# Sparse attention and four attention experts: 64-query blocks with one 120-row contraction, heads in pairs, batched small operations, stationary weights in the projections

## The chip, the cores and the metric

The kernel runs on one core of a Trainium2 chip. The metric is device time in microseconds of one launch; the kernel before took 674.88 us, the median of three runs (674.37 to 676.24). The engines are PE (matrix multiplications; it takes a stationary operand by a weight load and streams a moving one past it), DVE, ACT and POOL (elementwise work), and SP, which here only issues DMAs. Each engine has its own instruction stream and waits for others on semaphores. PE writes to PSUM, a small memory that DVE and ACT read.

## The reference

Two parts in sequence. The first is attention for 4 batches, 8 heads, 768 positions and 64 dimensions. Each query sees the keys less than 16 positions away, and 24 summaries of 32 keys each (the maximum of the keys, the mean of the values), whose scores get log(32) added:

```
k_sum = k.reshape(B, H, nb, block, D).max(axis=3)
v_sum = v.reshape(B, H, nb, block, D).mean(axis=3)
mask_l = np.abs(pos[:, None] - pos[None, :]) < window
scores_s = scale * np.einsum('bhsd,bhnd->bhsn', q, k_sum)
scores_s = scores_s + np.log(block)
scores_all = np.concatenate([scores_l_m, scores_s], axis=-1)
return np.matmul(a, v_all).astype(np.float32)
```

Its output, heads side by side, is x: 4 batches of 768 rows of 512. The second part picks two of four experts per row and adds their causal attention (64 dimensions each), weighted:

```
logits = x @ w_gate
topk = np.argpartition(-logits, K, axis=-1)[..., :K]
for e in range(E):
    q = x @ wq[e]; k = x @ wk[e]; v = x @ wv[e]
    ye = a @ v @ wo[e]
    out += mask[..., None] * w[:, :, kk:kk + 1] * ye
```

All four experts are computed for all rows, and the weight of an expert that isn't picked is zero. Since the choice compares logits, x has to be exact: both kernels compute the first part's values in f32 and carry x as the sum of two f16 numbers.

## The kernel before

**Stage 1** (L117 to L253) runs over batches and, inside, over four pairs of heads, and is done for all four batches before stage 2 begins. Per head: q, k and v are loaded (POOL issues q and k with a cast to f16, SP or ACT issues v in f32). PE transposes q and k, six tiles of 128 positions each (L145, L147), with 64 useful columns out of 128. Twelve records, six f32 matmuls with an indicator matrix (L155), give the sums of v over blocks of 32. For each tile of 128 queries there are two score matmuls: against the 128 keys of the tile itself (L182, mask by POOL, L193 and L195), and against a second set of 128 rows, `kT_B`, that holds neighbours of the tile and the 24 summaries (L185, mask by DVE, L197). ACT takes the exponential of both (L189). Two f32 matmuls of 128 stationary columns and 65 moving ones (64 values and a one for the sum of weights) add up the values (L205, L207); DVE and ACT divide, and split the result into a high and a low f16 part (L210 to L222). The twelve tiles of both parts are transposed (L238 to L248).

**Stage 2** (L255 to L402) runs per batch: the gate for each tile (thirteen small operations on 128 x 4 numbers), and for two pairs of experts the projection with x as stationary operand (L318), eviction, transposes of q and k (L327, L329), causal scores (L343), exponentials (L346, POOL clears above the diagonal), values (L357), division and weighting (L361 to L364); at the end the output projection (L392, L394) and the store.

**Order.** The program is written with a framework that orders the instructions of each engine by priority and readiness in its own model, sets semaphores, and hands out buffers from pools; a tile allocated again waits for the readers of the earlier one. PE's order in stage 1 interleaves the values of one head with the transposes and scores of the next. The number of buffers is written at each tile (`bufs=`).

## Time and profile before

| | us |
|---|---|
| median of three runs | 674.88 |
| lowest, highest | 674.37, 676.24 |
| span of the profiled execution | 676.0 |
| PE busy | 575.3 (85%) |
| DVE busy | 342.3 (51%) |
| ACT busy | 296.3 (44%) |
| POOL busy | 256.4 (38%) |

The profile is of one execution, whose own time is its span; it lies 1.1 us above the median. Busy shares are averages over both stages. The first stage ends at about 441 us. A matmul is pipelined: its duration contains the passage through the array, so what a matmul costs in a row of them is read from the distance of starts. A row of the timeline that merges several (x6) spans from the first start to the last end; less the duration of one, divided by their number less one, it gives that distance. An f32 matmul leaves two records, so x12 are six of them.

### The profile page before, as it was taken

How to read it: one execution, taken by the hardware profiler on the slowest of the kernel's cores; microseconds unless marked ns; L12 is line 12 of the kernel's file. 1: busy time of each engine (PE TensorE's matmuls, PEld its weight loads, DVE VectorE, ACT ScalarE, POOL GpSimd, SP SyncE). 2: the span in 40 equal slices, each digit the busy share in tenths (PEclk: the TensorE clock that was granted, in tenths of full speed). 3: DMA queues.
4: the chain of work that ended last, by engine and by line, in shares of the span. 5: the costliest groups of instructions: out<-in, count | busy, mean ns of one | idle time of the engine just before them, and what ended most of it. 6: DMA issues, size and time to landing. Idle time of an engine off the chain costs nothing.

```text
span 676.0 us, 10937 instructions
## 1 busy us (share of the span) xinstructions
PE 575.3 (85%) x3248; PEld 426.8 (63%) x3248; DVE 342.3 (51%) x1797; ACT 296.3 (44%) x958; POOL 256.4 (38%) x813
## 2 busy tenths in 40 slices
PE   1998999899998998999999898877887897797874
PEld 1887887788777877887778777653343343333331
DVE  0455554554554545545455455556565457447443
ACT  1444444444443444444444444434643643543541
POOL 9877453554544535545444243310210210210120
PEclk9999999999999999999999999999776566655655
DMA  5977241332322413323231010000001002002002
GB/s 66 60 67 60 36 35 18 35 39 23 30 24 37 36 17 34 39 25 29 25 42 19 13 24 1 1 1 0 1 33 62 1 1 95 0 1 84 12 1 93
DMA packets 85962, 20.63 MB, mean 31 GB/s; under 512 B 82576, under 2 KB 82832, under 8 KB 85904
## 3 DMA queue, kind: packets, MB, share of 16 engines
q0 software_dynamic: 56832, 7.35, 16.8%
q1 hardware_dynamic: 14800, 6.30, 3.4%
q10 hardware_dynamic: 14272, 6.29, 3.3%
q8 instruction: 26, 0.43, 0.3%
q14 instruction: 32, 0.26, 0.1%
HBM read 20.98 MB, written 6.29 MB: 40 GB/s over the span
## 4 chain that ended last, share of the span: by engine, by line
PE 75%; DVE 11%; ACT 7%; issue 3%; POOL 3%; DMA 0%; ACTq 0%; DVEq 0%; POOLq 0%
PE av_ps L205 15%; PE vs_ps L155 13%; PE av_ps L207 12%; PE pqkv_ps L318 7%; PE score_ps L343 6%; PE score_ps L182 4%; PE T_ps_q L145 4%; PE score_ps L185 3%; PE av_ps L357 2%; ACT a L346 2%; DVE T_q L150 2%; PE trans_ps L327 2%; ACT x_pair_hi L214 2%; ACT aT L189 2%; DVE recip L210 2%
## 5 line engine op out<-in xcount | busy, mean ns | idle before, releaser
L205 PE MATMUL av_ps<-v_nat,aT 128*128 128x65 f32 x384 | 126.9, 433 | 5.5 <-DVE x_pair_lo L222 4.6
L214 ACT ACTIVATE x_pair_hi<-av_ps,recip 128x64 f16<-128x64 f32 x192 | 58.7, 313 | 160.6 <-DVE recip L210 128.0
L205 PEld LDWEIGHTS av_ps<-v_nat,aT 128*128 128x128 f32 x384 | 99.5, 319 | 34.6 <-issue 26.8
L207 PE MATMUL av_ps<-v_B_all,aT 128*128 128x65 f32 x384 | 121.1, 417 | 0.0
L210 DVE RECIPROCAL recip<-av_ps 128x1 f32<-128x1 f32 x192 | 32.3, 168 | 171.1 <-PE av_ps L207 171.0
L207 PEld LDWEIGHTS av_ps<-v_B_all,aT 128*128 128x128 f32 x384 | 104.9, 333 | 0.0
L155 PE MATMUL vs_ps<-v_nat,indic_cat 128*128 128x65 f32 x384 | 92.0, 420 | 15.0 <-POOL v_nat L140 14.5
L155 PEld LDWEIGHTS vs_ps<-v_nat,indic_cat 128*128 128x128 f32 x384 | 86.9, 331 | 18.4 <-POOL v_nat L140 14.7
L193 POOL TENSOR_SCALAR_AFFINE_SELECT aT<-aT 128x128 f32<-128x128 f32 x192 | 63.5, 334 | 75.7 <-ACT aT L189 73.7
L349 POOL TENSOR_SCALAR_AFFINE_SELECT a<-a 128x128 f16<-128x128 f16 x96 | 28.2, 295 | 137.1 <-ACT a L346 129.2
L189 ACT ACTIVATE aT<-score_ps 128x256 f32<-128x256 f32 x192 | 66.7, 381 | 20.8 <-PE av_ps L207 18.8
L346 ACT ACTIVATE a<-score_ps 128x512 f16<-128x512 f32 (+3 forms) x128 | 54.3, 450 | 42.8 <-PE score_ps L343 30.9
L318 PE MATMUL pqkv_ps<-wqkvp,xT_hi 128*128 128x384 f16 x192 | 61.3, 429 | 1.0 <-DVE qkv_nat L312 0.5
L197 DVE TENSOR_TENSOR aT<-aT,mask_cat 128x128 f32<-128x128 f32 x192 | 59.9, 312 | 3.0 <-ACT aT L189 0.6
L182 PE MATMUL score_ps<-T_q,T_k 64*128 64x128 f16 x192 | 50.2, 295 | 11.4 <-ACT aT L189 11.4
L195 POOL TENSOR_SCALAR_AFFINE_SELECT aT<-aT 128x128 f32<-128x128 f32 x192 | 56.3, 296 | 8.8
L343 PE MATMUL score_ps<-qT_sb,kT_sb 64*128 64x512 f16 (+3 forms) x128 | 46.8, 417 | 6.3 <-DVE qT_sb L312 3.7
L222 DVE SCALAR_TENSOR_TENSOR x_pair_lo<-av_ps,recip2k,xhi32s 128x64 f16<-128x64 f32 x192 | 50.4, 274 | 1.3 <-ACT xhi32s L218 0.4
L185 PE MATMUL score_ps<-T_q,kT_B_all 64*128 64x128 f16 x192 | 49.8, 306 | 0.0
L357 PEld LDWEIGHTS <-a 128*128 128x128 f16 x336 | 25.1, 122 | 33.7 <-DVE wav L364 17.7
L361 DVE RECIPROCAL rec<-av_ps 128x1 f32<-128x1 f32 x96 | 16.0, 167 | 54.4 <-PE av_ps L357 53.7
L357 PE MATMUL av_ps<-qkv_nat,a 128*128 128x65 f16 x336 | 35.0, 233 | 8.5 <-DVE wav L364 4.1
(120 smaller groups left out, 958.9 us busy)
## 6 DMA issues: line engine op xcount, KB each, us to landing
v_nat<-in_v_dram ACTq DMA_DIRECT2D x16, 192.0 KB, 2.6
v_nat<-in_v_dram SPq DMA_DIRECT2D x16, 192.0 KB, 2.6
q_nat<-in_q_dram POOLq DMA_DIRECT2D x32, 96.0 KB, 3.0
k_nat<-in_k_dram POOLq DMA_DIRECT2D x32, 96.0 KB, 3.0
out_dram<-out_sb SPq DMA_DIRECT2D x12, 256.0 KB, 2.0
out_dram<-out_sb ACTq DMA_DIRECT2D x12, 256.0 KB, 2.2
wqkvp<-in_moe_wq_dram POOLq DMA_DIRECT2D x4, 64.0 KB, 2.9
wqkvp<-in_moe_wk_dram POOLq DMA_DIRECT2D x4, 64.0 KB, 2.9
```

What stands on the lines that cost most here:

```text
L155: nc.tensor.matmul(vs_ps, indic_cat[:, u, :], v_nat[:, u, 0:65], start=(u == 0), stop=(u == NT - 1))
L182: nc.tensor.matmul(score_ps[:, 2 * i, :], T_k[:, t, :], T_q[:, t, :], start=True, stop=True)
L185: nc.tensor.matmul(score_ps[:, 2 * i + 1, :], kT_B_all[:, t, :], T_q[:, t, :], start=True, stop=True)
L189: nc.scalar.activation(aT[:, 2 * i:2 * i + 2, :], score_ps[:, 2 * i:2 * i + 2, :], AF.Exp, scale=SCALE)
L193: nc.gpsimd.affine_select(loc, loc, [[-1, 128]], AL.is_ge, 0.0, base=15, channel_multiplier=1)
L205: nc.tensor.matmul(av_ps, aT[:, 2 * i, :], v_nat[:, tt, 0:65], start=True, stop=False)
L207: nc.tensor.matmul(av_ps, aT[:, 2 * i + 1, :], v_B_all[:, tt, :], start=False, stop=True)
L214: nc.scalar.activation(x_pair_hi[:, tt, cols], av_ps[:, 0:64], AF.Copy, scale=recip)
L318: nc.tensor.matmul(pp, xT_hi[b][ch][:, ti, :], wqkv_pair[cc][:, ch, :], start=(ch == 0), stop=(ch == NCH - 1))
L343: nc.tensor.matmul(sp[:, 0:G, :], kT_sb[ep][:, tj, :], qT_sb[ep][:, tj + j0:tj + j0 + G, :], start=True, stop=True)
L346: nc.scalar.activation(a2[:, j0:j0 + G, :], sp[:, 0:G, :], AF.Exp, scale=SCALE)
L357: nc.tensor.matmul(avp, a2_all[ep][tj][:, ti - tj, :], qkv_nat[ep][:, tj, 128:193], start=(tj == 0), stop=(tj == ti))
```

## The change

Stage 2 of a batch now follows stage 1 of the same batch. In stage 1 the unit of work is a pair of heads, whose 64 dimensions lie side by side on 128 partitions: q and k of both heads are transposed together. Queries go in twelve blocks of 64. For each block there is one set of 120 keys: 96 local ones (the block and 16 on each side, cut at the ends) and the 24 summaries. Scores are built in PSUM in three steps: a matmul with the identity adds the mask (-30000 outside the window, L171), 64-column matmuls add the local scores on rows 0 to 95 (L178), and wide ones add the summaries on rows 96 to 119 (L184). One exponential of 768 columns per head goes over all 120 rows (L188). The values then need one f32 matmul per block, with 64 stationary columns and a contraction of 120 rows (L196). The matching rows of v, `v_blk`, are put together by DMA: 96 rows per block from DRAM (L142, L145) and 24 sums copied to all blocks (L148). The sums come from `v_s`, four heads with a block of 32 rows in each of 96 partitions, by five halving additions on POOL (L123). The factor 32 for the logarithm sits in the column of ones. Division is one reciprocal and one multiplication per head, the transposes of x are six in f32 (L206), and the split into high and low parts follows after them (L209, L210).

In stage 2 the q and k projections hold the weights of two experts stationary and stream x (L268), so their result needs no transpose. Values of all experts and the gate's logits come from one matmul with 264 columns (L224). The gate's small operations run once per batch on 128 x 24 numbers. Exponentials, divisions and stores go over wider pieces.

```diff
...
+    maskb = consts.tile((128, NQ, 64), HALF, name="maskb")
+    nc.gpsimd.memset(maskb, 0.0)
...
+    v_bufs = [consts.tile((128, 2, NQ, 65), FP32, name=f"v_blk{i}") for i in range(NVB)]
+    for i in range(NVB):
+        nc.gpsimd.memset(v_bufs[i][:, :, :, 64:65], 1.0 / XS)
+        nc.gpsimd.memset(v_bufs[i][96:128, :, :, 64:65], 32.0 / XS)
...
-                    vs_ps = ps1.tile((128, 65), FP32, name="vs_ps", bufs=1)
-                    for u in range(NT):
-                        nc.tensor.matmul(vs_ps, indic_cat[:, u, :], v_nat[:, u, 0:65],
-                                         start=(u == 0), stop=(u == NT - 1))
...
-                            nc.gpsimd.affine_select(loc, loc, [[-1, 128]], AL.is_ge,
-                                                    0.0, base=15, channel_multiplier=1)
-                            nc.gpsimd.affine_select(loc, loc, [[1, 128]], AL.is_ge,
-                                                    0.0, base=15, channel_multiplier=-1)
-                            nc.vector.tensor_tensor(aT[:, 2 * i + 1, :],
-                                                    aT[:, 2 * i + 1, :],
-                                                    mask_cat[:, 1, :], AL.mult)
...
+            v_s = s1.tile((96, 2048), FP32, name="v_s", bufs=2)
+            nc.sync.dma_start(out=v_s,
+                              in_=v[b, 4 * g:4 * g + 4].rearrange("h (n s) d -> (h n) (s d)", s=32))
+            half = 1024
+            while half >= 64:
+                nc.gpsimd.tensor_tensor(v_s[:, 0:half], v_s[:, 0:half],
+                                        v_s[:, half:2 * half], AL.add)
+                half //= 2
...
+            for src, dst in ((q, q_nat), (k, k_nat)):
+                for hp in range(2):
                     nc.gpsimd.dma_start(
+                        out=dst[:, :, 64 * hp:64 * hp + 64],
+                        in_=src[b, 2 * c + hp].rearrange("(t p) d -> p t d", p=128))
+            v_blk = v_bufs[(NCH * b + c) % NVB]
+            vb = v[b, 2 * c:2 * c + 2]
+            for hp in range(2):
+                vh = v[b, 2 * c + hp]
+                src = bass.AP(vh.tensor, vh.offset + 48 * D,
+                              [[D, WIN], [64 * D, NQ - 2], [1, D]])
+                nc.sync.dma_start(out=v_blk[0:WIN, hp, 1:NQ - 1, 0:64], in_=src)
+                src = bass.AP(vh.tensor, vh.offset,
+                              [[D, WIN], [(S - WIN) * D, 2], [1, D]])
+                nc.sync.dma_start(out=v_blk[0:WIN, hp, 0:NQ:NQ - 1, 0:64], in_=src)
+                hh = 2 * (c % 2) + hp
+                vs = vsums[c // 2][NSUM * hh:NSUM * hh + NSUM, 0:64]
+                nc.sync.dma_start(out=v_blk[WIN:KR, hp, :, 0:64],
+                                  in_=vs.unsqueeze(1).to_broadcast((NSUM, NQ, 64)))
+            qT_ps = ps.tile((128, NT, 128), HALF, name="qT_ps", tag="one", bufs=4)
+            for t in range(NT):
+                nc.tensor.transpose(qT_ps[:, t, :], q_nat[:, t, :], ident16)
+            qT = s1.tile((128, S), HALF, name="qT", bufs=2)
+            nc.vector.tensor_copy(qT, qT_ps.rearrange("p t n -> p (t n)"))
+            kT_ps = ps.tile((128, NT, 128), HALF, name="kT_ps", tag="one", bufs=4)
+            for t in range(NT):
+                nc.tensor.transpose(kT_ps[:, t, :], k_nat[:, t, :], ident16)
+            kT = s1.tile((128, S), HALF, name="kT", bufs=2)
+            nc.vector.tensor_copy(kT, kT_ps.rearrange("p t n -> p (t n)"))
+            ksum = s1.tile((128, NSUM), HALF, name="ksum", bufs=2)
+            nc.vector.tensor_reduce(ksum, kT.rearrange("p (n w) -> p n w", w=32),
+                                    AX.X, AL.max)
+            aTs = []
+            sps = []
+            for hp in range(2):
+                sc = ps.tile((128, 1024), FP32, name="sc", tag="two", bufs=2)
+                sps.append(sc)
+                for lo, hi in ((0, 512), (512, 768)):
+                    nc.tensor.matmul(sc[:, lo:hi], ident16,
+                                     maskb.rearrange("p t n -> p (t n)")[:, lo:hi],
+                                     start=True, stop=False, skip_group_check=True)
+            for t in range(NQ):
                 for hp in range(2):
+                    rows = slice(64 * hp, 64 * hp + 64)
+                    w0 = win_start(t)
+                    nc.tensor.matmul(sps[hp][0:WIN, 64 * t:64 * t + 64],
+                                     kT[rows, w0:w0 + WIN], qT[rows, 64 * t:64 * t + 64],
+                                     start=False, stop=False, skip_group_check=True)
+            for hp in range(2):
+                rows = slice(64 * hp, 64 * hp + 64)
+                for lo, hi in ((0, 512), (512, 768)):
+                    nc.tensor.matmul(sps[hp][WIN:KR, lo:hi], ksum[rows, :], qT[rows, lo:hi],
+                                     start=False, stop=True, skip_group_check=True)
+            for hp in range(2):
+                aT = s1.tile((128, S), FP32, name="aT", bufs=4)
+                nc.scalar.activation(aT[0:KR, :], sps[hp][0:KR, 0:S], AF.Exp, scale=SCALE)
+                aTs.append(aT)
+            x32 = s1.tile((128, NT, 128), FP32, name="x32", bufs=2)
+            for hp in range(2):
+                av = ps.tile((128, NT, 65), FP32, name="av", tag="one", bufs=4)
+                for t in range(NQ):
+                    o = 64 * (t % 2)
+                    nc.tensor.matmul(av[o:o + 64, t // 2, :],
+                                     aTs[hp][0:KR, 64 * t:64 * t + 64],
+                                     v_blk[0:KR, hp, t, :], start=True, stop=True)
+                rec = s1.tile((128, NT, 1), FP32, name="rec", bufs=4)
+                nc.vector.reciprocal(rec, av[:, :, 64:65])
+                nc.vector.tensor_tensor(x32[:, :, 64 * hp:64 * hp + 64], av[:, :, 0:64],
+                                        rec.to_broadcast((128, NT, 64)), AL.mult)
+            xT_ps = ps.tile((128, 1024), FP32, name="xT_ps", tag="two", bufs=2)
+            for t in range(NT):
+                nc.tensor.transpose(xT_ps[:, 128 * t:128 * t + 128], x32[:, t, :], ident32)
+            hi = xpool.tile((128, S), HALF, name=f"xT_hi{c}", bufs=2)
+            lo = xpool.tile((128, S), HALF, name=f"xT_lo{c}", bufs=2)
+            nc.scalar.copy(hi, xT_ps[:, 0:S])
+            nc.vector.tensor_tensor(lo, xT_ps[:, 0:S], hi, AL.subtract)
...
+        for t2 in range(NT // 2):
+            vp = ps.tile((128, 2, 512), FP32, name="vp", tag="two", bufs=2)
+            for i in range(2):
+                cols = slice(128 * (2 * t2 + i), 128 * (2 * t2 + i) + 128)
+                for ch in range(NCH):
+                    nc.tensor.matmul(vp[:, i, 0:264], xT_hi[ch][:, cols], wvg[:, ch, :],
+                                     start=(ch == 0), stop=False, skip_group_check=True)
+                for ch in range(NCH):
+                    nc.tensor.matmul(vp[:, i, 256:264], xT_lo[ch][:, cols],
+                                     wvg[:, ch, 256:264],
+                                     start=False, stop=(ch == NCH - 1), skip_group_check=True)
+            for i in range(2):
+                nc.vector.tensor_copy(v2[:, 2 * t2 + i, :, 0:64],
+                                      vp[:, i, 0:256].rearrange("p (e d) -> p e d", e=E))
+            nc.vector.tensor_copy(lgp[:, 2 * t2:2 * t2 + 2, :], vp[:, :, 256:264])
...
+            qk = []
+            for j in range(2):
+                pp = ps.tile((128, 1024), FP32, name="pp", tag="two", bufs=2)
+                for lo, hi in ((0, 512), (512, 768)):
+                    for ch in range(NCH):
+                        nc.tensor.matmul(pp[:, lo:hi], wqk[:, ch, cc, j, :],
+                                         xT_hi[ch][:, lo:hi],
+                                         start=(ch == 0), stop=(ch == NCH - 1))
+                t = s2.tile((128, S), HALF, name=f"qkT{j}", bufs=2)
+                if j == 0:
+                    nc.vector.tensor_copy(t, pp[:, 0:S])
+                else:
+                    nc.scalar.copy(t, pp[:, 0:S])
+                qk.append(t)
+            a2s = [s2.tile((128, 2688), HALF, name="a2", bufs=4) for _ in range(2)]
+            for g, grp in enumerate(GROUPS):
+                for ep in range(2):
+                    rows = slice(64 * ep, 64 * ep + 64)
+                    sp = ps.tile((128, 1024), FP32, name="sp", tag="two", bufs=2)
+                    for tj, col in grp:
+                        n0 = 128 * tj
+                        while n0 < S:
+                            c0 = col + n0 - 128 * tj
+                            w = min(S - n0, 512 - c0 % 512)
+                            nc.tensor.matmul(sp[:, c0:c0 + w],
+                                             kT[rows, 128 * tj:128 * tj + 128],
+                                             qT[rows, n0:n0 + w], start=True, stop=True)
+                            n0 += w
+                    base, ln = GBASE[g], GLEN[g]
+                    nc.scalar.activation(a2s[ep][:, base:base + ln], sp[:, 0:ln], AF.Exp,
+                                         scale=SCALE / (XS * XS))
+                    step = grp[1][1]
+                    dg = bass.AP(a2s[ep].tensor, a2s[ep].offset + base,
+                                 [list(a2s[ep].ap[0]), [step, 2], [1, 128]])
+                    nc.gpsimd.affine_select(dg, dg, [[0, 2], [1, 128]], AL.is_ge, 0.0,
+                                            base=0, channel_multiplier=-1)
...
+                r2 = s2.tile((128, NT, 1), FP32, name="r2", bufs=4)
+                nc.vector.reciprocal(r2, av2[:, :, 64:65])
+                cmb = s2.tile((128, NT, 1), FP32, name="cmb", bufs=4)
+                nc.vector.tensor_tensor(cmb, r2, g_b[:, :, e:e + 1], AL.mult)
+                nc.vector.tensor_tensor(wav[:, :, 64 * ep:64 * ep + 64], av2[:, :, 0:64],
+                                        cmb.to_broadcast((128, NT, 64)), AL.mult)
...
+        x = stage1(b)
+        if b == 0:
+            load_stage2_weights()
+        stage2(b, *x)
```

Three places in the order of the instructions. The names: `q_nat`, `k_nat` are loaded q and k, `sc` and `score_ps` scores in PSUM, `av` and `av_ps` values in PSUM, `xT_ps` transposed x. In brackets stands the engine or DMA queue waited for.

First PE at the change of a pair. In the kernel before, in mid stage 1, values of one head, transposes of x, scores and sums of v of the next follow each other:

```order
L205 MATMUL av_ps<-v_nat,aT 128x65 [waits DVE_49,PE_49,Pool_49]
L207 MATMUL av_ps<-v_B_all,aT 128x65
...
L248 LDWEIGHTS x_pair_lo
L248 MATMUL xT_ps<-ident_98,x_pair_lo 128x128 [waits Activation_49]
...
L182 LDWEIGHTS T_k
L182 MATMUL score_ps<-T_q,T_k 128x128 [waits Activation_49]
L185 LDWEIGHTS kT_B_all
L185 MATMUL score_ps<-T_q,kT_B_all 128x128
...
L155 MATMUL vs_ps<-v_nat,indic_cat 128x65 [waits DMAHW4_49,Pool_49]
L155 MATMUL vs_ps<-v_nat,indic_cat 128x65 x5
```

After the change the same place reads, from the transposes of x of one pair to the values of the next:

```order
L206 MATMUL xT_ps<-ident_75,x_207 128x128 [waits DVE_49,PE_49]
L206 MATMUL xT_ps<-ident_75,x_207 128x128 x5
L171 LDWEIGHTS ident_70
L171 MATMUL sc<-maskb,ident_70 128x512 [waits PE_49]
...
L178 LDWEIGHTS kT [waits DVE_49]
L178 MATMUL sc<-qT,kT 96x64
...
L184 MATMUL sc<-qT,ksum 24x512
...
L171 MATMUL sc<-maskb,ident_70 128x512 [waits DVE_49]
...
L196 MATMUL av<-v_blk_108,aT 64x65 [waits DMAHW1_49,DMAHW2_49,Activation_49,Pool_49]
L196 MATMUL av<-v_blk_108,aT 64x65 [waits DMAHW6_49]
L196 MATMUL av<-v_blk_108,aT 64x65 x10
```

The sums of v are gone from PE and the values stand in one block. The mask of the second head waits for DVE, which has to read `xT_ps` of the pair before, since the tag `two` has two buffers.

Then POOL at the start. Before, its loads of q and k follow the fills:

```order
L114 MEMSET kT_B_all 64x768
L115 MEMSET v_B_all 128x390
L130 DMA q_nat<-in_q_dram 128x6x64
L133 DMA k_nat<-in_k_dram 128x6x64
L140 MEMSET v_nat 128x6
```

After, the additions of both halves of the heads stand ahead of the first load:

```order
L106 MEMSET v_blk_110 32x24
L123 TENSOR_TENSOR v_s<-v_s 96x1024 [waits DMAHW0_49]
L123 TENSOR_TENSOR v_s<-v_s 96x1024 [waits DMAHW1_49]
L123 TENSOR_TENSOR v_s<-v_s 96x512 [waits Pool_49] x2
L123 TENSOR_TENSOR v_s<-v_s 96x256 [waits Pool_49] x2
L123 TENSOR_TENSOR v_s<-v_s 96x128 [waits Pool_49] x2
L123 TENSOR_TENSOR v_s<-v_s 96x64 [waits Pool_49]
L133 DMA q_nat<-in_q_dram 128x6x64
```

Nine of the ten additions stand between the last fill and the first load, and the tenth right behind it.

Last SP's queue. Before, it held one load of v for every second head:

```order
L137 DMA v_nat<-in_v_dram 128x6x64 x2
L93 DMA wg_f_105<-in_moe_w_gate_dram 128x4x4
L137 DMA v_nat<-in_v_dram 128x6x64 [waits DMAHW0_49,PE_49,Activation_49]
L137 DMA v_nat<-in_v_dram 128x6x64 [waits DMAHW2_49,PE_49,Activation_49]
L137 DMA v_nat<-in_v_dram 128x6x64 [waits DMAHW1_49,DMAHW5_49,PE_49,Activation_49]
```

After, it holds six DMAs per pair of heads and two for `v_s` per batch:

```order
L119 DMA v_s<-in_v_dram 96x2048 x2
L142 DMA v_blk_107<-in_v_dram 96x10x64
L145 DMA v_blk_107<-in_v_dram 96x2x64
...
L148 DMA v_blk_107<-v_s 24x12x64 [waits DMAHW0_49,Pool_49]
L148 DMA v_blk_107<-v_s 24x12x64
L145 DMA v_blk_108<-in_v_dram 96x2x64 [waits DMAHW1_49]
L148 DMA v_blk_108<-v_s 24x12x64 [waits DMAHW2_49]
L142 DMA v_blk_108<-in_v_dram 96x10x64 [waits DMAHW3_49]
L145 DMA v_blk_108<-in_v_dram 96x2x64 [waits DMAHW4_49]
```

From the ninth DMA on each waits for the lane, one of eight, of an earlier one, and what copies sums waits for POOL too.

## Rows read from the trace of the kernel before

**Rows 1.** The page: span, then busy time, share and instructions of PE.

```profile
span 676.0 us, 10937 instructions
...
PE 575.3 (85%) x3248; PEld 426.8 (63%) x3248; DVE 342.3 (51%) x1797; ACT 296.3 (44%) x958; POOL 256.4 (38%) x813
```

**Rows 2.** The chain of waits, 100 to 170 us: start, us, what.

```profile
112.22 2.75 PE vs_ps L155 x12
...
139.09 2.75 PE vs_ps L155 x12
```

**Rows 3.** Stretches: length, busy by engine (count), PEclk, DMA share, GB/s.

```profile
112.20:139.10 26.90, 24.77 (x134) 21.58 (x133) 13.83 (x67) 12.14 (x42) 12.75 (x40) 1.00 0.30 30
460.00:662.00 202.00, 166.70 (x1049) 76.47 (x1049) 108.98 (x657) 94.18 (x304) 29.51 (x108) 0.64 0.07 24
```

**Rows 4.** Timeline of PE in stage 1: start, us, line, operation, out<-in, shape.

```profile
119.37 0.63 PE L207 MATMUL av_ps<-v_B_all,aT 128*128 128x65 f32 x2
...
120.02 0.31 PE L182 MATMUL score_ps<-T_q,T_k 64*128 64x128 f16 x1
...
120.36 0.69 PE L205 MATMUL av_ps<-v_nat,aT 128*128 128x65 f32 x2
...
218.50 0.63 PE L205 MATMUL av_ps<-v_nat,aT 128*128 128x65 f32 x2
218.93 0.63 PE L207 MATMUL av_ps<-v_B_all,aT 128*128 128x65 f32 x2
219.36 0.63 PE L248 MATMUL xT_ps<-ident,x_pair_lo 128*128 128x128 f16 x4
```

**Rows 5.** The chain of waits, 441 to 470 us, the projections.

```profile
452.43 1.62 PE pqkv_ps L318 x5
...
465.09 0.83 PE pqkv_ps L318 x5
```

**Rows 6.** Groups of DVE by shape: count, busy us, mean ns, idle before.

```profile
L158 DVE TENSOR_REDUCE kT_B_all<-T_k 64x24 f16<-64x768 f16 x32 | 29.8, 930 | 0.0
...
L150 DVE COPY T_q<-T_ps_q 64x768 f16<-64x768 f16 x32 | 17.3, 540 | 18.0 <-PE T_ps_q L145 17.7 <-PE score_ps L185 0.2
...
L210 DVE RECIPROCAL recip<-av_ps 128x1 f32<-128x1 f32 x192 | 32.3, 168 | 171.1 <-PE av_ps L207 171.0
...
L398 DVE COPY out_sb<-out_ps 128x512 f32<-128x512 f32 x12 | 8.3, 691 | 5.6 <-PE out_ps L394 5.6
```

**Rows 7.** Groups of ACT by shape.

```profile
L346 ACT ACTIVATE a<-score_ps 128x512 f16<-128x512 f32 x48 | 28.7, 597 | 28.6 <-PE score_ps L343 19.0 <-PE av_ps L357 9.0
...
L346 ACT ACTIVATE a<-score_ps 128x128 f16<-128x128 f32 x32 | 8.9, 278 | 1.3 <-PE score_ps L343 0.8
```

**Rows 8.** Timeline of the start, all engines.

```profile
0.81 0.35 POOL L45 MEMSET indic_cat<- 128x128 f32 x2 [0.29 <-POOLq L417]
...
8.26 0.40 POOL L69 COPY mask_cat<-mask_cat 128x256 f32<-128x256 f32 x1
...
12.10 0.95 POOL L130 DMA_DIRECT2D q_nat<-in_q_dram  x1
13.05 0.84 POOL L133 DMA_DIRECT2D k_nat<-in_k_dram  x1
...
16.25 0.84 PE L145 MATMUL T_ps_q<-ident,q_nat 128*128 128x128 f16 x6
```

**Rows 9.** DMA, 100 to 300 us: queues, then issues with KB and us to landing.

```profile
q0 software_dynamic: 22232, 2.79, 21.9%
q10 hardware_dynamic: 6272, 1.57, 3.4%
...
q_nat<-in_q_dram POOLq DMA_DIRECT2D x15, 96.0 KB, 3.0
...
v_nat<-in_v_dram SPq DMA_DIRECT2D x7, 192.0 KB, 2.6
```

More of the change, by code (lines that the diff above doesn't have):

```diff
@@ L4 @@
 import concourse.tile as tile
-from concourse import bass_utils, mybir
+from concourse import mybir
 from concourse._compat import with_exitstack
@@ L19, with win_start @@
 NT = 6
+NQ = 12
 NCH = 4
 E = 4
+WIN = 96
+NSUM = 24
+KR = WIN + NSUM
 SCALE = 0.125
+XS = 256.0
 LO_SCALE = 2048.0
-INV_LO = 1.0 / 2048.0
+NEG = -30000.0
+GROUPS = [[(0, 0), (4, 768)], [(1, 0), (3, 640)], [(2, 0), (5, 512)]]
+GBASE = [0, 1024, 2048]
+GLEN = [1024, 1024, 640]
+OFF2 = {tj: GBASE[g] + col for g, grp in enumerate(GROUPS) for tj, col in grp}
+def win_start(t):
+    return min(max(64 * t - 16, 0), S - WIN)
 @with_exitstack
@@ new lines @@
+    ps = ctx.enter_context(tc.tile_pool(name="ps", bufs=2, space=bass.MemoryType.PSUM))
+    ident16 = consts.tile((128, 128), HALF, name="ident16")
+    make_identity(nc, ident16)
+    ident32 = consts.tile((128, 128), FP32, name="ident32")
+    make_identity(nc, ident32)
+    maskb = consts.tile((128, NQ, 64), HALF, name="maskb")
+    nc.gpsimd.memset(maskb, 0.0)
+    for t0, t1 in ((0, 1), (1, NQ - 1), (NQ - 1, NQ)):
+        shift = 64 * t0 - win_start(t0)
+        m = maskb[0:WIN, t0:t1, :]
+        n = t1 - t0
+        nc.gpsimd.affine_select(m, m, [[0, n], [-1, 64]], AL.is_ge, NEG,
+                                base=15 - shift, channel_multiplier=1)
+        nc.gpsimd.affine_select(m, m, [[0, n], [1, 64]], AL.is_ge, NEG,
+                                base=15 + shift, channel_multiplier=-1)
@@ L406 @@
+    for b in range(B):
+        x = stage1(b)
+        if b == 0:
+            load_stage2_weights()
+        stage2(b, *x)
 _INS = ['q', 'k', 'v', 'moe_w_gate', 'moe_wq', 'moe_wk', 'moe_wv', 'moe_wo']
```

414 lines of the change are left out of this document (94 added, 320 removed).

## The prediction, made before the changed kernel ran

> **What bounds the kernel now.** I read the page from the top. The span is 676.0 us and PE is busy 575.3 of it [rows 1]. PE alone does not say which stage is limited by what, so next came the chain of waits: in the first stage the same piece, `vs_ps` L155 x12, comes back after 26.9 us, once per pair of heads [rows 2]. Sixteen pairs make 430 us; with the start the first stage ends near 441 us, ahead of the projections at 452 [rows 5], and the second takes the rest. The view by stretches shows PE busy 24.77 of those 26.9 us, DVE 13.8, ACT 12.1, POOL 12.8 [rows 3]: the first stage is bound by PE.
>
> At what clock? The column PEclk reads 1.00 there [rows 3], but durations contradict it. Four 128-column transposes take 0.63 us, the last 0.31 of it being one instruction's own length, so a start comes every 0.107 us [rows 4]: 128 columns in 0.107 us is the lower level, 1.2 GHz. Likewise five 384-column projections follow each other in the chain at 0.32 us each at 452 us (1.62/5), and at 0.17 each at 465 us (0.83/5) [rows 5]: only there is it 2.4 GHz. So the whole first stage ran at 1.2 GHz, although PE was 92% busy. From 460 to 662 us the mean granted clock is 0.64 [rows 3], that is (0.64-0.5)/0.5 = 28% of the time at the higher level.
>
> In the first stage the 128x65 f32 matmul is the dear one: two records, and the next instruction 0.43 us after the first [rows 4]. [...] Thirty-six of them (L155, L205, L207) are 15.4 us of a pair's 26.9.
>
> **The change, stage 1, per pair, at the lower level.** Removed are L155 (12 f32 matmuls, 5.1 us), half of the q/k transposes, and all work of POOL and DVE on `aT`. What PE then does:
> - 12 transposes x 0.107 = 1.3 us.
> - 4 mask and 4 summary matmuls, 3072 columns at 0.107 per 128 = 2.6 us.
> - 24 scores of 64 columns: 0.053 each by columns, 0.107 if the 96 stationary columns set it; I take 0.08, 1.9 us (1.3 to 2.6).
> - 24 f32 matmuls with 64 stationary columns. No row has this form. From above, the nearest row: 0.43 each, 10.3 us. From below: two halves of the array side by side, 0.108 each, 2.6 us. [...]
> - 6 f32 transposes: 0.107 to 0.43 each, I take 0.21, 1.3 us (0.6 to 2.6).
> - Changes between 128 and 64 rows. L207 to the next L205 across three scores takes 0.99 us [rows 4] where 0.43 + 3 x 0.107 = 0.75 would do: 0.24 for in and out. Three such excursions, 0.7 us (0 to 1.4).
>
> Sum 13.0 us (8.4 to 20.8 with all ends together). DVE is left with two copies (0.54 each), the reduce (0.93), the reciprocals, the two multiplications and one subtract of 768 columns from PSUM; from 1 column at 0.17 and 512 at 0.69 [rows 6] a column is 1.02 ns, so 0.56 and 0.95 us, in all 4.4 us. ACT has two exps and a copy of 768 columns: 512 take 0.60 and 128 take 0.28 [rows 7], so 768 take 0.81, in all 2.4 us. Both hide under 13.
>
> **The new wait.** In the order the second mask matmul (L171) waits for DVE, for the subtract of the pair before, because `sc` and `xT_ps` share two PSUM buffers. Behind it on PE stand 12 scores and two summary matmuls, and for these ACT's second exp waits. From the last f32 matmul of a pair: reciprocal 0.17 and multiplication 0.56, transposes, copy 0.81, subtract 0.95, then mask, 12 scores and summaries, exp 0.81, the 12 f32 matmuls of the second head, and some 0.8 for eight hand-overs. At the lower level that is 0.73+1.3+0.81+0.95+2.2+0.81+2.6+0.8 = 10.2 us, less than PE's 13.0, so it is covered. At the higher level the PE parts halve and it is 7.1 us, against PE's (13.0-0.7)/2+0.7 = 6.9: nothing covers it, and I take 8 for the pair.
>
> **Stage 2, per batch.** Columns on PE: values with gates 6528, projections 12288, scores 10752, 84 x 65 = 5460, transposes 1536, output 6144; 42,700, that is 35.6 us at the lower and 17.8 at the higher level. The path alternates between engines, though. At the lower level: values 5.4; for each of the two expert pairs projections 5.1, copy 0.8, first scores 0.8, exps of 5376 columns in six pieces 5.5 (ACT), last values 1.2, normalizing 0.9, transposes 0.6, copy 0.8, hand-overs 0.6, together 16.3; output and the first wait 8. Sum 46. At the higher level 3.3 + 2 x 12.5 + 3.7 = 32, since ACT and DVE do not get faster. Before it is (676-441)/4 = 59 us. The gate operations go from 13 per tile to 12 per batch and lie beside the projections.
>
> **Which level?** The first stage stays as it is in kind (f32 matmuls, short f16 ones), and the second has the projections that stood ahead of the higher level in [rows 5]. I take the 28% of the time that [rows 3] show, for both: a pair 1/(0.28/8+0.72/13.0) = 11.1 us, a batch 1/(0.28/32+0.72/46) = 41 us.
>
> **Start and end.** Before, POOL's 39 fills, selections and copies run from 0.81 us until the first q load is issued at 12.10, 0.29 each, and the first transpose starts at 16.25 [rows 8]. After, 21 such instructions (6 us) come, and then on POOL, ahead of the first q load, the ten adds of L123. No row has an add on POOL; a copy of 256 columns takes 0.40 [rows 8], by which 2 x 1984 columns take 6.2 us; as pure per-instruction cost 10 x 0.2 = 2. I take 6.2, the row per column. Then four issues (0.84 each) and 3.0 to landing [rows 8, 9]: 0.8+6+6.2+3.4+3.0 = 19.4 us. [...] The end: the last store, costed at the 2.6 us to landing of [rows 9], 3 us with what lies around.
>
> **Sum.** 19.4 + 16 x 11.1 + 4 x 41 + 3 = 364 us. The span shown is 676.0 and the median of the runs 674.88, so 1 us lies between them; I leave it. DMA: one pair moves 3072 packets of q and k at 1.97 ns (21.9% of 200 us over 22,232) and 2880 for `v_blk` plus some 1500 for the sums at 1.08 ns (3.4% over 6272) [rows 9]: 10.8 us of all sixteen engines, 43 per batch out of 85, and buffers for three or four pairs let it run on in stage 2. I cost it at nothing.
>
> **Rivals.**
> - A: the lower level throughout, as the first stage of before. 19.4 + 16 x 13.0 + 4 x 46 + 3 = 414 us. For it: 430 us at 92% busy without one rise. Against it: stage 2 now follows each batch.
> - B: the higher level mostly: 19.4 + 128 + 128 + 3 = 278, with a fifth of the time lower about 300. For it: less stationary load between columns. It would also come of the halves side by side (2.6 us less in a pair). [...]
> - C: the 64-column form is no cheaper, 0.43 each: a pair 18.1 at the lower level, 19.4 + 290 + 184 + 3 = 496 us. For it: the only f32 rows there are.
> - D: SP's queue. Six `v_blk` DMAs stand one behind another on it for each pair. If each had to land (2.6 us [rows 9]) before the next, 15.6 us per pair: 436 us.
> - E, slower than before: the same queue with dearer transfers. L148 spreads the sums from SBUF to 24 partitions; if the six take over 5.1 us each, twice the row, and nothing overlaps, a pair is above (675-19-164-3)/16 = 30.5 us and the gain is gone. Against it: loads of 192 KB land in 2.6, and eight may be under way.
>
> **Chances.** Forecast 0.45 (its own range 325 to 400), A 0.18, B 0.2, C 0.08, D 0.06, E 0.03. The range 290 to 440 leaves out C, E and the lower part of B, together under 0.2. Within 0.3% is what can't be told from no change here; only a small part of E falls there. Faster 0.96, same 0.01, slower 0.03.
>
> **What would show it.** The starts of L178 and L196: 0.08 and 0.217 us apart at the lower level. L171's second matmul: if it idles for DVE more than 1 us per pair, the new wait is not covered. Pair to pair 11 us, batch to batch some 85. First transpose at about 19 us. If PE idles for `v_blk`, it is D; for POOL's adds at each batch, the start's price comes four times. The forecast is wrong if the level is other than a mix, or if the f32 form costs 0.43.

## The result and the profile after

The changed kernel takes 300.25 us, the median of four runs (295.64 to 302.71); against the kernel before the ratio is 0.4414 (0.438 to 0.4448). Its time moves with the mean granted clock (295.64 us at 0.874, 302.71 at 0.843), and ratios here and below leave out runs that fell far behind the best of their kernel. The time lies in the range, at its low end: what came is rival B, to which the prediction gave 0.2, not the forecast of 364 us.

The page of the changed kernel, as in [rows 1], and then three stretches with the columns of [rows 3]: three pairs of the second batch, the second stage of that batch, and the second stage of the first batch.

```profile
span 298.8 us, 5906 instructions
...
PE 218.1 (73%) x2448; PEld 140.8 (47%) x2448; DVE 123.0 (41%) x280; ACT 96.0 (32%) x117; POOL 127.1 (43%) x191
```

```profile
104.20:126.40 22.20, 19.95 (x320) 14.65 (x320) 12.85 (x25) 7.87 (x10) 12.11 (x13) 1.00 1.62 215
126.40:164.40 38.00, 30.52 (x263) 18.36 (x264) 16.55 (x45) 14.02 (x18) 16.14 (x26) 0.78 0.42 69
55.30:101.60 46.30, 30.99 (x248) 18.26 (x249) 19.86 (x41) 14.88 (x18) 28.17 (x39) 0.74 0.74 83
```

From the values of one pair to those of the next are 7.2 us, where one pair took 26.9 (the first stretch holds three such pairs and 0.7 us more). Cut at the value matmuls of the first stage, both spans divide without a remainder:

| us | before | after |
|---|---|---|
| until the first value matmul | 26.7 | 29.5 |
| first to last (after: in the four batches together) | 422.2 | 93.9 |
| the rest: second stages, with the changes between the stages | 227.1 | 175.4 |

So 328 of the 377 us are the first stage's, and 52 come from the rest, although it now holds the first transposes and scores of three batches too. The start takes 3 us more.

The timeline of PE, as in [rows 4]: the first transposes, scores and values of all, then values and transposes of the second batch.

```profile
21.94 0.80 PE L153 MATMUL qT_ps<-ident,q_nat 128*128 128x128 f16 x6 [15.67 <-DMA q_nat<-in_q_dram]
...
26.69 1.17 PE L178 MATMUL sc<-qT,kT 64*96 64x64 f16 x24 [0.65 <-DVE kT L160]
...
29.55 2.87 PE L196 MATMUL av<-v_blk,aT 120*64 120x65 f32 x48 [0.94 <-issue]
...
104.17 1.62 PE L196 MATMUL av<-v_blk,aT 120*64 120x65 f32 x48 [0.95 <-ACT aT L188]
105.72 0.51 PE L153 MATMUL qT_ps<-ident,q_nat 128*128 128x128 f16 x6
106.06 0.50 PE L158 MATMUL kT_ps<-ident,k_nat 128*128 128x128 f16 x6
```

Six transposes in 0.51 us, one of them 0.22: a start every 0.058 us, the higher level. At 21.94 the distance is about 0.1, the lower, 0.107 in [rows 4]. Where the prediction and the expectations write 1.2 and 2.4 GHz, these two paces are what the rows show: 128 columns in 0.107 and in 0.058 us, 1.2 and 2.2 columns a ns. In the trace the transposes of q are at the lower level in 4 of the 16 pairs: the first two, and the first of the third and fourth batch, which stand among the last matmuls of a second stage. The value matmuls are at the lower level in the first pair alone. At the higher level they need (1.62-0.22)/47 us per record and so, with two records, 0.06 each. The same 24 at the lower level take 2.87 us, 0.11 each: the lower bound of the prediction, not the 0.217 it took. The 24 scores at 26.69, at the lower level too, take 1.1 us until the next row starts, below the 1.3 that the prediction had as their least.

The chain of one pair, with the columns of [rows 2]:

```profile
112.03 0.97 PE av L196 x24
...
113.25 0.56 DVE x L201
113.81 0.46 DVE qT L155
114.27 0.48 DVE kT L160
...
114.77 0.95 DVE ksum L162
115.73 0.91 DVE xT_lo L210
...
116.68 0.49 PE sc L171 x2
117.17 0.65 PE sc L178 x12
117.82 0.44 PE sc L184 x2
...
118.34 0.82 ACT aT L188
...
119.20 0.97 PE av L196 x24
```

From 112.03 to 119.20 are 7.17 us, and the way holds the predicted new wait: the second mask (L171) follows the subtract (L210). PE is busy some 90% of the time beside it. It idles only 0.41 us a pair for the subtract, less than the 1 us that the prediction named as a sign, and the wait sets the pace all the same. Before the subtract the chain goes through DVE's copies and reduce (L155 to L162), which the prediction had not put there. The way that it had, through the transposes of x and ACT's copy, ends at 115.64 us, the reduce at 115.72: the two are equally late. Last the start, as in [rows 8], and the same additions a batch later:

```profile
6.61 2.33 POOL L123 TENSOR_TENSOR v_s<-v_s 96x1024 f32<-96x1024 f32 x1 [1.29 <-DMA v_s<-in_v_dram]
...
9.42 7.23 POOL L123 TENSOR_TENSOR v_s<-v_s 96x1024 f32<-96x1024 f32 x8 [0.48 <-DMA v_s<-in_v_dram]
16.59 0.99 POOL L133 DMA_DIRECT2D q_nat<-in_q_dram  x1
```

```profile
66.33 10.83 POOL L123 TENSOR_TENSOR v_s<-v_s 96x1024 f32<-96x1024 f32 x10
77.11 1.12 POOL L298 TENSOR_SCALAR_AFFINE_SELECT a<-a 128x256 f16<-128x256 f16 x3
```

```profile
59.24 1.04 PE L224 MATMUL vp<-wvg,xT_hi 128*128 128x264 f16 x4 [3.09 <-DMA wvg<-in_moe_wv_dram]
...
77.57 0.29 PE L307 MATMUL av<-v,a 128*128 128x65 f16 x2 [5.04 <-POOL a L298]
```

The first load of q goes out at 16.59 us, later than before (12.10). At 66.33 the ten additions, themselves behind POOL's loads for the next pairs, take 10.8 us, and the masks of the second stage stand behind them: PE waits 5.0 us for the first. Earlier it waits 3.1 us for weights of this stage that land late. So the first batch's second stage is some 8 us longer than the second's. In the second batch the additions end before the first mask is wanted.

### The profile page after: what moved, and what is told of

The parts are those of the page before. It is cut to its first block, busy times and chain, and to the rows that moved or that the text cites. A ratio compares the mean times of both kernels' runs of the same rounds, so it can differ in the third digit from the quotient of the medians.

```text
span 298.8 us, 5906 instructions
## 1 busy us (share of the span) xinstructions
PE 218.1 (73%) x2448; PEld 140.8 (47%) x2448; DVE 123.0 (41%) x280; ACT 96.0 (32%) x117; POOL 127.1 (43%) x191
## 4 chain that ended last, share of the span: by engine, by line
PE 46%; DVE 22%; ACT 12%; POOL 9%; DMA 5%; issue 4%; SPq 0%; ACTq 0%; POOLq 0%
PE sp L288 7%; PE pp L268 6%; POOL v_s L123 6%; PE av L196 6%; PE av L307 6%; DVE xT_lo L210 5%; ACT a L293 4%; PE op L325 4%; PE sc L178 4%; ACT aT L188 4%; DVE ksum L162 4%; DVE x L201 4%; PE vp L224 3%; PE sc L171 3%; DMA v_s<-in_v_dram 3%
## 5 line engine op out<-in xcount | busy, mean ns | idle before, releaser
L298 POOL TENSOR_SCALAR_AFFINE_SELECT a<-a 128x256 f16<-128x256 f16 x48 | 19.4, 406 | 102.5 <-ACT a L293 102.5
L293 ACT ACTIVATE a<-sp 128x1024 f16<-128x1024 f32 (+1 forms) x48 | 41.2, 921 | 13.4 <-PE sp L288 13.4
L188 ACT ACTIVATE aT<-sc 120x768 f32<-120x768 f32 x32 | 25.5, 810 | 54.3 <-PE sc L184 54.3
L133 POOL DMA_DIRECT2D q_nat<-in_q_dram x32 | 26.9, 850 | 36.8 <-PE qT_ps L153 31.6
L123 POOL TENSOR_TENSOR v_s<-v_s 96x1024 f32<-96x1024 f32 (+4 forms) x40 | 40.6, 1023 | 3.4 <-DMA v_s<-in_v_dram 1.8
L288 PE MATMUL sp<-qkT,qkT 64*128 64x512 f16 (+3 forms) x128 | 27.8, 364 | 19.0 <-ACT a L293 10.4
L196 PE MATMUL av<-v_blk,aT 120*64 120x65 f32 x768 | 29.8, 231 | 5.1 <-ACT aT L188 2.9
L196 PEld LDWEIGHTS av<-v_blk,aT 120*64 120x64 f32 x768 | 25.9, 143 | 12.4 <-ACT aT L188 7.0
L307 PE MATMUL av<-v,a 128*128 128x65 f16 x336 | 25.5, 242 | 5.1 <-POOL a L298 5.0
L209 ACT CAST xT_hi<-xT_ps 128x768 f16<-128x768 f32 x16 | 12.8, 798 | 47.4 <-PE xT_ps L206 47.4
L133 POOL DMA_DIRECT2D k_nat<-in_k_dram x32 | 26.7, 854 | 1.5 <-DMA k_nat<-in_k_dram 1.5
L268 PE MATMUL pp<-xT_hi,wqk 128*128 128x512 f16 (+1 forms) x128 | 27.0, 358 | 0.0
L178 PEld LDWEIGHTS <-kT 64*96 64x96 f16 x384 | 18.8, 126 | 10.4 <-issue 5.7
L171 PE MATMUL sc<-maskb,ident 128*128 128x512 f16 x64 | 16.1, 337 | 10.3 <-DVE xT_lo L210 5.0
L178 PE MATMUL sc<-qT,kT 64*96 64x64 f16 x384 | 22.3, 212 | 0.6 <-DVE kT L160 0.6
L224 PE MATMUL vp<-wvg,xT_hi 128*128 128x264 f16 x96 | 19.1, 342 | 4.8 <-DMA wvg<-in_moe_wv_dram 3.1
```

The source lines that it names most:

```text
L123: nc.gpsimd.tensor_tensor(v_s[:, 0:half], v_s[:, 0:half], v_s[:, half:2 * half], AL.add)
L133: nc.gpsimd.dma_start(out=dst[:, :, 64 * hp:64 * hp + 64], in_=src[b, 2 * c + hp].rearrange("(t p) d -> p t d", p=128))
L171: nc.tensor.matmul(sc[:, lo:hi], ident16, maskb.rearrange("p t n -> p (t n)")[:, lo:hi], start=True, stop=False, skip_group_check=True)
L178: nc.tensor.matmul(sps[hp][0:WIN, 64 * t:64 * t + 64], kT[rows, w0:w0 + WIN], qT[rows, 64 * t:64 * t + 64], start=False, stop=False, skip_ ...
L188: nc.scalar.activation(aT[0:KR, :], sps[hp][0:KR, 0:S], AF.Exp, scale=SCALE)
L196: nc.tensor.matmul(av[o:o + 64, t // 2, :], aTs[hp][0:KR, 64 * t:64 * t + 64], v_blk[0:KR, hp, t, :], start=True, stop=True)
```

## The experiments

**The value matmul with 128 stationary columns** (the even blocks then get the rows of v of the odd ones).

```diff
-                    nc.tensor.matmul(av[o:o + 64, t // 2, :],
-                                     aTs[hp][0:KR, 64 * t:64 * t + 64],
+                    nc.tensor.matmul(av[:, t // 2, :],
+                                     aTs[hp][0:KR, 64 * t - o:64 * t - o + 128],
```

> The changed kernel, but each value matmul (L196) holds 128 stationary columns (two blocks of weights) and writes 128 rows; 24 of them per pair as before, so the even blocks come out wrong: that part is changed. The changed kernel takes 300 us, 7.2 us a pair in the first stage at the higher TensorE level. Theory L: what kept the first stage of the old kernel at 1.2 GHz was the weight load of 128 f32 columns, during which little streams. Then the level falls again (128-column f16 transposes 0.107 us apart), the 24 cost 0.43 each = 10.3 us, the rest of the pair 2 x 5 us: about 20 us a pair, 300 + 16 x 13 = 505 us. Theory M: the 512-column mask and summary matmuls hold the higher level, whatever the f32 form. Then the transposes stay 0.055 apart, the 24 cost 0.213 each = 5.1 us, a pair is about 10 to 11 us and the total 345 to 360 us.

401 to 424 us (granted 0.75 to 0.70), between the two. Timeline of PE:

```profile
123.08 9.51 PE L196 MATMUL av<-v_blk,aT 120*128 120x65 f32 x48 [0.95 <-ACT aT L188]
132.39 0.84 PE L153 MATMUL qT_ps<-ident,q_nat 128*128 128x128 f16 x6
...
138.23 5.57 PE L196 MATMUL av<-v_blk,aT 120*128 120x65 f32 x48
143.64 0.50 PE L153 MATMUL qT_ps<-ident,q_nat 128*128 128x128 f16 x6
...
148.99 5.57 PE L196 MATMUL av<-v_blk,aT 120*128 120x65 f32 x48
```

Now 10 of 16 pairs have their transposes at the lower level (four in the changed kernel). In one pair the 24 cost 0.39 each on average and leave the level low, in the next 0.23 at the higher. Neither theory alone: with the wide f32 weights the level falls often, and in the rest of the pair it comes back. The two prices can be told apart: the pair that keeps the higher level takes 10.8 us (138.23 to 148.99), 3.6 more than in the changed kernel, 57 us in sixteen pairs. What the run takes beyond that, over 40 us, goes with the level: the pair whose values run at the lower one takes 15.2 us (123.08 to 138.23).

**No mask matmuls** (the mask is left out).

```diff
-                for lo, hi in ((0, 512), (512, 768)):
-                    nc.tensor.matmul(sc[:, lo:hi], ident16,
...
-                                     start=False, stop=False, skip_group_check=True)
+                                     start=True, stop=True, skip_group_check=True)
```

> The changed kernel without the four mask matmuls of a pair (L171); the mask is left out, scores start their own sums. Theory M (the wide f16 matmuls of the mask hold the higher level): the level falls in the first stage, 2 x 5.3 us of PE a pair, about 10.6 us, total about 355 us. Theory L (the f32 weight load was what held it low): the level stays; the second mask matmul stood in the chain with 0.49 us between the release of its buffer and the scores, so a pair goes from 7.2 to about 6.7 us, total 290 to 293 us.

300.24 us, ratio 0.4431 (0.4402 to 0.446): the same, with 1 us of PE less in every pair.

```profile
37.40 1.89 PE L192 MATMUL av<-v_blk,aT 120*64 120x65 f32 x48
...
44.06 1.95 PE L192 MATMUL av<-v_blk,aT 120*64 120x65 f32 x48
...
110.97 2.72 PE L192 MATMUL av<-v_blk,aT 120*64 120x65 f32 x48
113.63 0.82 PE L153 MATMUL qT_ps<-ident,q_nat 128*128 128x128 f16 x6
...
118.49 1.95 PE L192 MATMUL av<-v_blk,aT 120*64 120x65 f32 x48
120.38 0.51 PE L153 MATMUL qT_ps<-ident,q_nat 128*128 128x128 f16 x6
```

Where the level holds, a pair takes 6.7 us (37.40 to 44.06), the 0.5 us less that theory L worked out. But the level falls and returns from pair to pair (7 of 16 low and one in part, granted 0.80 to 0.82 against 0.84 to 0.87), and a pair like that at 110.97 takes 7.5. So in these runs the level is held better with the mask matmuls than without, and their PE time is paid back by it; L's 290 us was wrong, and M's 355 as well. Whether it is their width or only that PE has more to do isn't told apart.

**Values in another order**, the six even blocks first, then the six odd ones.

```diff
-                for t in range(NQ):
+                for t in list(range(0, NQ, 2)) + list(range(1, NQ, 2)):
```

> The changed kernel with the twelve value matmuls of a head in another order: first the six even blocks, which all write partitions 0 to 63, then the six odd ones, partitions 64 to 127. Nothing is computed otherwise. [...] Both heads stand on the way of a pair at least in part: 0.6 to 1.2 us a pair, total 310 to 320 us. Rival: the form costs 0.058 by itself, and nothing changes (within 1%).

306.49 us, ratio 0.4542 (0.4511 to 0.4572), 9 us more by the ratios. The chain:

```profile
102.42 2.49 PE av L196 x48
...
110.15 2.42 PE av L196 x48
...
117.82 3.93 PE av L196 x48
```

24 in one half after the other cost 2.42 us, 0.10 each instead of 0.06 (1.62 us for the 24): two that alternate between the halves take 0.12 us, little longer than one of a row in the same half, so by these times two blocks overlap in the changed kernel. Shown by the same work in another order; which part of a matmul overlaps isn't. The total is just under the expectation, and here too the level falls at times (3.93).

**The old order of the stages.**

```diff
-        x = stage1(b)
+        xs.append(stage1(b))
...
+    for b in range(B):
+        stage2(b, *xs[b])
```

> The changed kernel with the old order of the stages: the first stage of all four batches, then the second of all four (buffers of x for four batches). Theory D: the transfers of a pair take more than its 7.2 us (by the queues' shares in the changed kernel some 11 to 14 us of all sixteen engines), and are hidden only because the second stage of each batch, which loads nothing, gives them time. Then the first stage runs at the pace of the transfers, 11 to 14 us a pair, and the total is 355 to 400 us. Rival: the loads have room, a pair stays at 7.2 us, total 295 to 303 us.

324.52 us, ratio 0.4809 (0.4782 to 0.4836). That lies between the two expectations. Within a batch D is wrong: a pair still takes 7.2 us (130.10 to 137.27). The values of ten of sixteen pairs run at the higher level, so the old order of the stages alone doesn't bring the lower one back. What is late stands between the batches, in the chain:

```profile
109.45 2.38 POOL v_s L123
...
116.98 4.34 DMA v_blk<-v_s
...
121.46 1.57 PE av L196 x24
```

The additions stand in POOL's queue behind loads that wait for PE, then come 5.4 us per half and the copies. The second stage in between hides that. Transfers have a part in it: the copies land after 4.34 us, and ahead of the second batch the chain also holds 13.7 us until a load of weights lands. D's price was wrong, but the transfers aren't free.

**The kernel before without its sums of v** (the summaries' values are changed).

```diff
-                    for u in range(NT):
-                        nc.tensor.matmul(vs_ps, indic_cat[:, u, :], v_nat[:, u, 0:65],
...
+                    nc.vector.tensor_copy(v_B_all[64:88, 0, :], v_nat[64:88, 0, 0:65])
```

> The kernel before without the twelve f32 matmuls per pair that sum v (L155); the rows of the summaries are copied from v instead, so the summaries' values are changed. If the first stage is bound by PE at the lower level, as the rows of before say, a pair loses 12 x 0.427 = 5.1 us: 675 - 82 = 593 us, and the 128-column transposes stay 0.107 us apart since 24 f32 matmuls with 128 stationary columns are left. Rival: the level rises with less f32 work in the mix: a pair falls towards 12 to 14 us, total 460 to 500 us. Rival: other engines' chains set the pair: less than 40 us gained.

628.62 us, ratio 0.9304 (0.926 to 0.9348), 47 us. A pair:

```profile
108.04:131.91 23.87, 20.20 (x111) 16.57 (x109) 14.02 (x66) 12.33 (x41) 12.71 (x40) 1.00 0.34 35
```

```profile
108.48 0.84 PE L147 MATMUL T_ps_k<-ident,k_nat 128*128 128x128 f16 x6
```

3.0 of the 5.1 us come through, then PE waits (20.2 of 23.9 busy) and the level stays low, as in the first expectation; the total lies above its 593 us. PE was the bound, but other engines' chains stood 2 us behind it.

**An earlier start**: in the first batch q and k of the first pair are loaded ahead of the additions, and these run on DVE.

```diff
+        if b == 0:
+            load_qk(0)
...
-                nc.gpsimd.tensor_tensor(v_s[:, 0:half], v_s[:, 0:half],
+                eng = nc.vector if b == 0 else nc.gpsimd
```

> The changed kernel (300 us) with another start: in the first batch the loads of q and k of the first pair are issued ahead of the additions for the sums of v, and these additions run on DVE; later batches as they were. In the changed kernel PE has its first scores at 26.7 us and the values start at 29.5; the ten additions hold POOL from 6.6 to 17.9 us and again from 66.3 to 77.2 us, where the masks of the second stage (L298) stand behind them. Theory P (POOL's additions are what is late at both places): first scores at about 15 us and values at 18, 11 us gained; the weights and the loads for the second batch are issued earlier too, so that most of the 8 us by which the first batch's second stage is longer than the others' (46 against 38) goes as well: 281 to 286 us. Rival Q: the start is bound by the transfers (all sixteen engines are taken from 1 to 26 us), q and k land no earlier than before or v_blk comes late instead; gain 0 to 4 us, 296 to 300 us.

286.70 us, ratio 0.4247 (0.4228 to 0.4267), just above P's 281 to 286. P holds for the start:

```profile
14.79 1.17 PE L189 MATMUL sc<-qT,kT 64*96 64x64 f16 x24 [0.65 <-DVE kT L171]
...
17.65 3.10 PE L207 MATMUL av<-v_blk,aT 120*64 120x65 f32 x48 [0.94 <-issue]
...
46.64 1.57 PE L207 MATMUL av<-v_blk,aT 120*64 120x65 f32 x24 [3.26 <-DMA v_blk<-v_s]
```

Scores start at 14.8 instead of 26.7 us. From the last values of the first batch to the next values are 43.4 us instead of 50.0. But rival Q's late `v_blk` came as well: in the first batch the values wait for the copied sums in three pairs, 5.6 us together. From first to last they take 30.6 us there instead of 24.6, which takes back most of what the second stage gained.

**Projections first in the second stage**, the values a third after each group of scores.

```diff
+            qT, kT = proj(cc)
...
+                if cc == 0:
+                    values(g)
```

> The changed kernel with the second stage in another order: the q and k projections of the first two experts and their first scores come first, the values and gate logits (L224 to L259) one third after each group of scores. Theory: the second stage (38 us a batch) is a chain between engines; the values matmuls (3 us of it) wait for the subtract of the last pair (L210, 1 us) and the projections stand behind them. In the new order both lie beside the exponentials: 3 to 4 us a batch, 284 to 289 us. Rival: PSUM has two large buffers, and the values now take turns with the scores in them, so that PE waits for evictions there: nothing gained or up to 2 us a batch lost, 298 to 308 us.

292.58 us, ratio 0.4297 (0.4263 to 0.433): a gain, between the two expectations. In the second and third batch, from the last values to the next are 37.8 us instead of 40.5 and 41.8. In the first they are 53.4 instead of 50.0, since the masks, wanted earlier, stand behind the same additions:

```profile
74.59 0.29 PE L316 MATMUL av<-v,a 128*128 128x65 f16 x2 [10.94 <-POOL a L303]
```

**Both.**

> Both edits together, the early start and the projections first. If both gains are there and independent, 300 - 15 - 14 = 271 us (267 to 277). If the transfers bound the start, only the second gain remains, about 286 us.

282.98 us, ratio 0.4177 (0.4154 to 0.4201), less than the sum of both. The stretches from the last values of the first and of the last batch on, with the columns of [rows 3], and a mask of the first and of the second batch:

```profile
46.40:94.10 47.70, 34.79 (x270) 20.16 (x270) 15.58 (x46) 16.17 (x20) 20.76 (x30) 0.71 0.75 101
239.00:281.70 42.70, 30.95 (x228) 17.25 (x226) 13.32 (x40) 15.17 (x18) 4.88 (x12) 0.74 0.10 38
```

```profile
61.50 0.29 PE L327 MATMUL av<-v,a 128*128 128x65 f16 x2 [4.44 <-POOL a L314]
...
125.13 0.41 POOL L314 TENSOR_SCALAR_AFFINE_SELECT a<-a 128x256 f16<-128x256 f16 x1 [0.21 <-ACT a L309]
```

In the first batch PE still waits for masks behind the additions, 4.4 us for the first, and the stretch is 4.3 us longer than with the early start alone. In the second and third batch the mask waits for ACT, not for POOL, and the stretches take 37.8 us as with the projections first alone. The last, without any additions, takes 4.8 us more than there, at a granted clock of 0.74 against 0.91.

**Both, with all additions on DVE** (`eng = nc.vector`).

> The kernel with both edits (early start, projections first; 283 us), with all additions for the sums of v on DVE (L123 of the changed kernel). In that kernel the masks of the second stage (L298) wait behind ten additions on POOL (10.9 us) in batches two and three, and the projections-first order brings the scores that need them forward. Theory: POOL's additions are what took back part of the two gains (14 + 8 expected as 22, 17 measured); on DVE the ten take 6.0 us (measured in the early start) and lie beside the values' evictions: 272 to 278 us. Rival: DVE's own queue then delays the evictions and the gate by the 6 us per batch: 281 to 288 us.

276.93 us at first, ratio 0.4056 (0.4034 to 0.4077). The expectation names the wrong place, batches two and three; what POOL's additions held up is the first.

> The fastest version once more (early start, projections first, all additions on DVE), for a narrower interval and a profile at the clock that its faster runs had (granted 0.90 against 0.72 in the profile of the first time, which took 289.6 us). 272 to 280 us.

278.76 us over six runs (271.20 to 286.52), ratio 0.4032 (0.4022 to 0.4042). In the profile, of a run of 272.56 us, the first batch's stretch takes 39.8 us at a granted 0.91, with both edits alone it took 47.7 at 0.71. This version is faster than both kernels.

**Both, with the additions a batch ahead on POOL.**

> The same with the additions on POOL but loaded and issued a batch ahead, during the first stage of the batch before, with two more buffers for v_s. If POOL then does them where it waits for PE anyway, 272 to 278 us; where they still fall among the masks of the second stage, 279 to 284 us.

293.16 us, ratio 0.4336 (0.4311 to 0.436): worse than without, and both expectations were wrong. The additions still stand among the masks, but PE waits only 4.4 us for masks in all, and 4.5 us for copied sums in the first batch. What else is longer stands at a lower clock: the second stages of the first two batches take 46.7 and 46.8 us at a granted 0.71 and 0.69, that of the third 38.0 at 0.87. Why it fell there stays open.

**The copy of k on ACT.**

```diff
-            nc.vector.tensor_copy(kT, kT_ps.rearrange("p t n -> p (t n)"))
+            nc.scalar.copy(kT, kT_ps.rearrange("p t n -> p (t n)"))
```

> The changed kernel (300 us, 7.17 us a pair) with the copy of k transposed (L160) on ACT instead of DVE. In the chain of a pair DVE does copies, reduce and subtract one after the other, and the second mask matmul (L171) waits for the subtract. Theory DVE: DVE's order is what is late, so 0.5 us a pair goes: 292 us. Rival: the subtract starts at 115.67, right when ACT's high part is done (115.64) and the reduce too (115.72); the way through transposes, high part and subtract is as long, so at most 0.1 us a pair is gained: 298 to 301 us.

300.85 us in the best of four runs, 311 to 313 in the others: no gain, unclear beyond that. In the trace the second mask now waits for the first exponential instead of the subtract:

```profile
111.38 1.95 PE L196 MATMUL av<-v_blk,aT 120*64 120x65 f32 x48
...
117.47 0.48 PE L171 MATMUL sc<-maskb,ident 128*128 128x512 f16 x2 [0.96 <-ACT aT L188]
...
118.96 1.95 PE L196 MATMUL av<-v_blk,aT 120*64 120x65 f32 x48
```

At the higher level a pair takes 7.58 us, 0.4 more than before the edit. So more changed than the place of the copy, and the run doesn't settle what DVE's order alone costs.

## Why the prediction was right, and where it was wrong

- **Direction and range**: right. The bound was PE at the lower level (transposes 0.107 us apart): without the sums of v a pair lost 3.0 us, of 5.1 worked out. With 128 stationary columns again, over 100 us of the gain are gone. The remaining parts of the first stage's gain, and all of the second stage's, were taken apart by no run. That the range held the result is owed to its width: it took in most of rival B, and the mix of levels that was forecast did not come.
- **The step that failed is "Which level?"**: it carried 28% of the time at the higher level from the second stage of before over to the first of after, because the work "stays as it is in kind". The kind had changed: the value matmuls of fifteen of sixteen pairs run at the higher level, 0.06 us each. A pair took 7.2 us instead of 11.1, which makes about 62 of the 64 us between forecast and result; 50 of them are the level's by the prediction's own 8 us for a pair at the higher one. The transposes are at the lower level in four pairs; with 128 f32 columns in ten, without the wide mask matmuls in seven. Which property of the work the clock follows isn't settled by these runs.
- **The value matmul** was mis-sized: 0.217 us at the lower level was taken, 5.2 us of a pair's 13.0. No run shows this term; the 24 took 2.87 us at the lower level, 0.11 each, and 1.62 at the higher, 0.06. The side-by-side halves stood in the bounds and in rival B; 0.06 us in turn against 0.10 in one half after the other agrees. Behind the 0.6 to 1.2 us a pair of the expectation for that order stands 0.6 us a head, which no run shows either: the 24 took 0.8 us more, 0.4 a head, and a pair 7.7 us instead of 7.2. The scores were too dear as well, 1.9 us taken and 1.1 measured at the lower level.
- **The new wait**: the pace was right, the way in part. 7.1 us by the chain were worked out, 7.17 measured; 8 had been taken. That the numbers meet so closely is partly luck: DVE's copies and reduce, 1.9 us, stand on the measured way and not in the sum, and the value matmuls were cheaper than in it.
- **Second stage**: 41 us taken, 38 measured at a granted 0.78; from batch to batch 63.7 and 64.9 us (first values to first values), where some 85 were expected. **The first batch's** 46 were missed: the queue behind POOL's additions was priced at the start alone, and the 3.1 us for the weights not at all.
- **Start**: the first transposes at 21.94 us, where 19.4 were taken, and the first scores at 26.69. The additions began at 6.61 us, as in the sum, but take 10.2 us instead of 6.2, and the loads land after 5.3 us (q) and 6.5 (k) instead of 3.0. The sum took a column of an addition at the price of the copy, 1.6 ns (0.40 us for 256); here 1024 take 2.33 us, 2.3 ns a column, and the small additions cost more than that by column (0.31 us for 64).
- **Transfers at nothing**: D and E, which put them at 436 us and more, fell. But they show in places: in the late weights and landings above, and in the values' waits for copied sums after the early start.

## What to carry to other kernels

Read the TensorE level from distances of starts, and don't carry it over from one kernel to the next: fewer stationary f32 columns gave back twice here, in the matmul (0.06 us each against 0.23 with 128 columns, both at the higher level) and in the level (transposes at the lower one in four pairs against ten). An operation moved to an idle engine cost here also what stood behind it in that engine's queue: the ten additions on POOL delayed loads at the start (the first to 16.59 us, from 12.10) and masks in the first batch's second stage (PE waited 5.0 us for the first). Gains that only add up on paper are worth one run together, and a missing part is looked for stretch by stretch, with the granted clock beside it.

## What the runs showed of the hardware that was not expected

By their times, two 64-column f32 matmuls that write different halves of the partitions overlapped: at the higher level 0.06 us each in turn, 0.10 when six of a half follow each other. The level changed with small changes of the work: without four mask matmuls in a pair, seven pairs had their transposes at the lower level (0.107 us apart) instead of four.
